# Half-depth products of the first expert layer made full-depth

## The chip, the cores and the metric

The kernel runs on one core of a Trainium2 chip. Its time is the device time of one execution in microseconds (us); runs of the kernel before gave 363.95, 364.14 and 370.61 us, median 364.14. "Faster" and "slower" in this document mean a difference of over 2%.

## The reference: what is computed

Two layers follow each other. First an mLSTM attention over 4 batches, 8 heads, 768 steps and head dimension 40, with a running maximum of the gates, a 40x40 state `C` and a normalizer `n`:

```python
C = f_stab * C + i_stab * einsum('bhd,bhe->bhde', vt, kt)
y[:, :, t] = sigmoid(o_gate) * (C @ qt) / max(|n . qt|, 1)
```

Its result, with heads side by side, is `x` of 4 x 768 rows and 320 columns. Then a gated expert layer:

```python
h = maximum(x @ w_in, 0)            # 320 -> 1024
u, v = h[..., :512], h[..., 512:]
v_n = (v - mean(v)) / sqrt(var(v) + 1e-6)
v_s = einsum('ts,bsd->btd', w_spatial, v_n) + b_spatial[None, :, None]
return (u * v_s) @ w_out            # 512 -> 320
```

The change lies in `x @ w_in`, the first expert layer.

## The kernel before, in words

**High and low parts.** TensorE multiplies a rounded form of float32 here (the type `F32R`). To keep accuracy each operand is split into a high part (a rounded copy) and a low part (what the rounding left): `xH` and `xL` for `x`, `wiH` and `wiL` for `w_in`, and likewise for the spatial weights (`wsH`, `wsL`) and the output weights (`woH`, `woL`). A product of two such operands is the sum of three: high with high, high with low, low with high, all added into one bank of the accumulator memory (PSUM). The product of the two low parts is left out.

**The depth of 320.** The sum over the 320 columns of `x` runs in blocks of 128 rows of the array: two full ones (`j` = 0, 1) and a third of 64 rows. The third is packed: line 655 (`xd`) copies the last 64 columns of `x` beside themselves, so that after the transposes (`px`, line 653) rows 0 to 63 and rows 64 to 127 of the third block of `xH` and `xL` hold the same values. Of the weights, `wiH`'s third block holds for the u half of the layer (columns 0 to 511) high parts in rows 0 to 63 and low parts in rows 64 to 127, and for the v half (columns 512 to 1023) high parts in rows 64 to 127 and low parts in rows 0 to 63. One product of `xH` with all 128 rows so gives two terms at once. The third term, low with high, needs only the 64 rows that hold the high weights. That is the half-depth product, the last of the eight that `a_terms` (line 660) lists.

**Who uses it.** `a_v` (line 675) makes the v half: for each batch and each block of 128 steps one group of eight products of 512 columns into `pm` (line 692), with `x` as the weights that are loaded into the array. `b_u` (line 717) makes the u half: for each batch, each half of the steps and each 128 columns of u one group of eight products of 384 columns into `pu` (line 734), with `w_in` as the loaded weights. That is 24 and 32 groups, so 56 half-depth products in all.

**The rest of TensorE's work.** `s` (line 539) scores, `ex` and `eb` (lines 542, 551) exponents of the gates, `dc` (lines 578, 580) state updates, `pv` (lines 606, 607) the attention's result, `px` transposes, `pb` (lines 744 to 746) the product with the spatial weights, three per block of 128 steps, and `pc` (lines 767 to 769) the output layer. `s`, `dc` and `pv` use narrower tiles of the array: `s` and `dc` 64 x 64, `pv` 128 x 64.

**The order of the work.** The table `ORDER` (lines 49 to 105) lists every task by name, in the order in which it is recorded; each engine runs its own tasks in that order, and semaphores hold back a task whose inputs are not there. `V..` are the `pm` groups, `pu...` the `pu` groups. Attention of later batches runs between the expert layers of earlier ones. DVE (VectorE) and ACT (ScalarE) empty PSUM and make the low parts; POOL (GpSimd) helps with both; SP and ACT issue the transfers. There are eight PSUM banks for all groups.

Of the kernel before, what the change touches and what calls it, by code (L numbers as in the profile page):

```python
# [24 lines left out]
DH = DFF // 2  # L25
# [16 lines left out]
    wiH=([128, 3, DFF], F32R), wiL=([128, 2, DFF], F32R), wsH=([128, 2, NB, 384], F32R), wsL=([128, 2, NB, 384], F32R),  # L42
# [164 lines left out]
class Kernel:  # L207
# [452 lines left out]
    def a_terms(self, b, hf, cx, cw):  # L660
        xH, xL = self.xT[b, hf]
        xH, xL = xH.t, xL.t
        wiH, wiL = self.F("wiH").t, self.F("wiL").t
        for j in range(2):
            yield xH[:, j, cx], wiH[:, j, cw]
            yield xH[:, j, cx], wiL[:, j, cw]
            yield xL[:, j, cx], wiH[:, j, cw]
        yield xH[:, 2, cx], wiH[:, 2, cw]
        r = slice(64, 128) if cw.start >= DH else slice(0, 64)
        yield xL[r, 2, cx], wiH[r, 2, cw]  # L670

    def wi_parts(self, hf):
        return [(self.F("wiH"), (hf, j)) for j in range(3)] + [(self.F("wiL"), (hf, j)) for j in range(2)]
# [164 lines left out]
```

## Time and profile before

| | |
|---|---|
| median of 3 runs | 364.14 us |
| the profiled execution | 364.62 us |
| its span, first to last instruction | 362.8 us |
| TensorE (PE) busy | 345.7 us, 3654 matmuls |
| weight loads (PEld) busy | 300.0 us |
| DVE, ACT, POOL busy | 256.5, 130.7, 108.2 us |

An instruction that the program calls a matmul is two in the trace: a load of the weights into the array (LDWEIGHTS, the PEld rows) and the streaming of the other operand (MATMUL, the PE rows). A load can run beside the matmul ahead of it. The profile models the ends of matmuls, so that neighbouring ones overlap in it, and a PE that reads as always busy may still have air in it. What a matmul costs in a dense stretch is read from the starts: from its own start to the next one's.

### The profile page before, as it was taken

How to read it: one execution, taken by the hardware profiler on the slowest of the kernel's cores; microseconds unless marked ns; L12 is line 12 of the kernel's file. 1: busy time of each engine (PE TensorE's matmuls, PEld its weight loads, DVE VectorE, ACT ScalarE, POOL GpSimd, SP SyncE). 2: the span in 40 equal slices, each digit the busy share in tenths (PEclk: the TensorE clock that was granted, in tenths of full speed). 3: DMA queues.
4: the chain of work that ended last, by engine and by line, in shares of the span. 5: the costliest groups of instructions: out<-in, count | busy, mean ns of one | idle time of the engine just before them, and what ended most of it. 6: DMA issues, size and time to landing. Idle time of an engine off the chain costs nothing.

```text
span 362.8 us, 9069 instructions
## 1 busy us (share of the span) xinstructions
PE 345.7 (95%) x3654; PEld 300.0 (83%) x3654; DVE 256.5 (71%) x545; ACT 130.7 (36%) x312; POOL 108.2 (30%) x154
## 2 busy tenths in 40 slices
PE   0599999999999999999999999999999999999996
PEld 0486877799998978799899878899999788898995
DVE  6899998789978877855487937677847666426362
ACT  2364675851530455622122145630112336302011
POOL 6132635654931042334321006420404412100000
PEclk9999999999999999999999999999999999999999
DMA  7779476966463752513405553160160000100012
GB/s 203 217 216 259 146 199 175 240 150 200 154 178 111 174 117 78 164 33 89 134 18 157 164 98 107 64 176 16 33 152 13 3 0 20 55 2 0 0 38 72
DMA packets 17866, 40.12 MB, mean 111 GB/s; under 512 B 4212, under 2 KB 7860, under 8 KB 17824
## 3 DMA queue, kind: packets, MB, share of 16 engines
q1 hardware_dynamic: 12048, 26.49, 26.9%
q10 hardware_dynamic: 5616, 12.94, 12.9%
q8 instruction: 29, 0.48, 0.6%
q0 software_dynamic: 160, 0.11, 0.2%
q14 instruction: 13, 0.11, 0.1%
HBM read 35.09 MB, written 4.42 MB: 109 GB/s over the span
## 4 chain that ended last, share of the span: by engine, by line
PE 92%; DMA 4%; DVE 2%; POOL 1%; issue 0%; ACT 0%; POOLq 0%; ACTq 0%
PE pm L692 15%; PE pu L734 14%; PE pb L744 11%; PE pb L746 9%; PE pb L745 9%; PE s L539 6%; PE pv L606 6%; PE pc L767 4%; PE dc L578 4%; PE pc L769 4%; PE pc L768 4%; PE px L653 3%; PE ex L542 2%; PE pv L607 1%; DMA GM<-in_gm 1%; DMA GM<-gp 1%
## 5 line engine op out<-in xcount | busy, mean ns | idle before, releaser
L744 PE MATMUL pb<-wsH,v 128*128 128x384 f32 x192 | 68.3, 356 | 0.2 <-DVE KS L255 0.2
L746 PE MATMUL pb<-wsH,v 128*128 128x384 f32 x192 | 64.7, 337 | 0.0
L745 PE MATMUL pb<-wsL,v 128*128 128x384 f32 x192 | 64.7, 337 | 0.0
L744 PEld LDWEIGHTS pb<-wsH,v 128*128 128x128 f32 x192 | 36.1, 188 | 5.6 <-issue 5.4
L539 PE MATMUL s<-QK 40*64 40x64 f32 x768 | 29.6, 233 | 9.7 <-DMA QK<-in_qk 9.7
L255 DVE TENSOR_TENSOR pb<-pb,bsp 128x384 f32<-128x384 f32 x32 | 17.7, 562 | 28.8 <-PE pb L746 28.7
L255 DVE TENSOR_TENSOR KS<-s,W 64x512 f32<-64x512 f32 x48 | 33.0, 687 | 5.6 <-PE s L539 3.3
L745 PEld LDWEIGHTS pb<-wsL,v 128*128 128x128 f32 x192 | 36.2, 189 | 0.3
L746 PEld LDWEIGHTS pb<-wsH,v 128*128 128x128 f32 x192 | 36.1, 188 | 0.0
L734 PE MATMUL pu<-xL,wiH 128*128 128x384 f32 (+1 forms) x96 | 35.5, 370 | 0.0
L539 PEld LDWEIGHTS s<-QK 40*64 40x64 f32 x768 | 26.4, 145 | 10.1 <-DMA QK<-in_qk 9.7
L734 PE MATMUL pu<-xH,wiH 128*128 128x384 f32 x96 | 33.1, 345 | 0.0
L692 PE MATMUL pm<-wiH,xL 128*128 128x512 f32 (+1 forms) x72 | 31.5, 438 | 0.0
L767 PE MATMUL pc<-woH,gt 128*128 128x320 f32 x96 | 31.2, 325 | 0.0
L259 ACT CAST gt<-pb 128x384 fp32r<-128x384 f32 x21 | 10.0, 480 | 58.8 <-DVE pb L255 51.0
L692 PE MATMUL pm<-wiH,xH 128*128 128x512 f32 x72 | 30.4, 422 | 0.0
L255 POOL TENSOR_TENSOR KS<-QK,Eb 64x512 f32<-64x512 f32 (+1 forms) x21 | 27.6, 1316 | 8.6 <-PE pc L769 7.0
L769 PE MATMUL pc<-woH,gt 128*128 128x320 f32 x96 | 29.7, 309 | 0.0
L768 PE MATMUL pc<-woL,gt 128*128 128x320 f32 x96 | 29.7, 309 | 0.0
L606 PE MATMUL pv<-RH,KS 104*64 104x41 f32 x384 | 27.3, 238 | 0.0
L607 PE MATMUL pv<-RH,KS 128*64 128x41 f32 x384 | 27.1, 238 | 0.1
L606 PEld LDWEIGHTS pv<-RH,KS 104*64 104x64 f32 x384 | 25.2, 145 | 2.1 <-issue 1.2
(124 smaller groups left out, 760.2 us busy)
## 6 DMA issues: line engine op xcount, KB each, us to landing
RH<-in_vk SPq DMA_DIRECT2D x35, 256.0 KB
QK<-in_qk SPq DMA_DIRECT2D x15, 448.0 KB
QK<-in_qk ACTq DMA_DIRECT2D x9, 448.0 KB
RH<-in_vk ACTq DMA_DIRECT2D x13, 256.0 KB
out<-o SPq DMA_DIRECT2D x14, 160.0 KB
wsr<-in_w_sp SPq DMA_DIRECT2D x5, 384.0 KB
out<-o ACTq DMA_DIRECT2D x10, 160.0 KB
wir<-in_w_in SPq DMA_DIRECT2D x3, 512.0 KB
```

Source lines behind the costliest of these rows:

```text
L255: return lambda e: e.tensor_tensor(out=out(), in0=in0(), in1=in1(), op=op)
L539: self.nc.tensor.matmul(o[64 - p0:128 - p0, h], q[p0:p0 + D, 0, h], q[p0:p0 + D, 1, h], start=True, stop=True)
L606: self.nc.tensor.matmul(o[0:64, h], ks[0:ke, 0, h], v0[0:ke, h], start=True, stop=True)
L607: self.nc.tensor.matmul(o[64:128, h], ks[:, 1, h], v1[:, h], start=True, stop=True)
L692: self.nc.tensor.matmul(pmt(), l, r, start=i == 0, stop=i == len(terms) - 1)
L734: self.nc.tensor.matmul(put(), w, x, start=i == 0, stop=i == len(terms) - 1)
L744: self.nc.tensor.matmul(pbt(), vH[:, cd], wh[:, s], start=s == 0, stop=False)
L745: self.nc.tensor.matmul(pbt(), vH[:, cd], wl[:, s], start=False, stop=False)
L746: self.nc.tensor.matmul(pbt(), vL[:, cd], wh[:, s], start=False, stop=s == NB - 1)
L767: self.nc.tensor.matmul(pct(), gH[:, c], wh[:, d], start=d == 0, stop=False)
L768: self.nc.tensor.matmul(pct(), gH[:, c], wl[:, d], start=False, stop=False)
L769: self.nc.tensor.matmul(pct(), gL[:, c], wh[:, d], start=False, stop=d == 3)
```

## The change

The half-depth product runs over all 128 rows of the third block. The rows that it now takes in hold the same low parts of `x` and the low parts of the weights, so that low times low is added for these 64 columns of `x`. It holds for both users of `a_terms`.

```diff
@@ a_terms
             yield xH[:, j, cx], wiL[:, j, cw]
             yield xL[:, j, cx], wiH[:, j, cw]
         yield xH[:, 2, cx], wiH[:, 2, cw]
-        r = slice(64, 128) if cw.start >= DH else slice(0, 64)
-        yield xL[r, 2, cx], wiH[r, 2, cw]
+        yield xL[:, 2, cx], wiH[:, 2, cw]
```

The number of instructions stays, and on each engine they stand in the same order. TensorE's instructions wait for the same semaphores at the same places. On the transfer queues a few transfers report to another of the eight completion semaphores than before, and one transfer on ACT's queue and one shift on DVE no longer carry a wait of their own.

## Rows read from the trace of the kernel before

**Rows 1.** The profile's page, totals and the chain that ended last.
```profile
PE 345.7 (95%) x3654; PEld 300.0 (83%) x3654; DVE 256.5 (71%) x545; ACT 130.7 (36%) x312; POOL 108.2 (30%) x154
...
PE 92%; DMA 4%; DVE 2%; POOL 1%; issue 0%; ACT 0%; POOLq 0%; ACTq 0%
```

**Rows 2.** Busy time by stretch: stretch, us, PE, PEld, DVE, ACT, POOL, clock, DMA.
```profile
20.00:50.00 30.00, 29.91 (x456) 22.77 (x456) 28.57 (x60) 17.92 (x44) 13.52 (x15) 1.00 0.80 212
50.00:75.00 25.00, 25.00 (x265) 19.61 (x264) 19.22 (x45) 18.28 (x45) 13.89 (x20) 1.00 0.77 192
75.00:100.00 25.00, 25.00 (x335) 23.54 (x334) 23.87 (x48) 9.64 (x21) 14.94 (x14) 1.00 0.57 169
100.00:125.00 25.00, 25.00 (x314) 22.86 (x312) 20.77 (x51) 6.29 (x15) 4.35 (x6) 1.00 0.54 147
125.00:150.00 25.00, 25.00 (x289) 20.23 (x288) 20.42 (x43) 13.44 (x35) 8.17 (x16) 1.00 0.43 106
```

**Rows 3.** All waits of PE from 50 us to the end: total, times, longest.
```profile
PE pb L744 <- DVE KS L255: 0.2, 1, 0.2
```

**Rows 4.** PE's groups by shape: rows*columns of the tile, moving operand, count, busy, mean ns.
```profile
L734 PE MATMUL pu<-xL,wiH 128*128 128x384 f32 x64 | 21.5, 337 | 0.0
...
L734 PE MATMUL pu<-xL,wiH 64*128 64x384 f32 x32 | 14.0, 436 | 0.0
...
L692 PE MATMUL pm<-wiH,xL 128*128 128x512 f32 x48 | 19.4, 403 | 0.0
...
L692 PE MATMUL pm<-wiH,xL 64*128 64x512 f32 x24 | 12.2, 507 | 0.0
```

**Rows 5.** The same for weight loads; last, idle time before them and what ended it.
```profile
L734 PEld LDWEIGHTS pu<-xL,wiH 128*128 128x128 f32 x64 | 12.0, 188 | 0.0
...
L734 PEld LDWEIGHTS pu<-xL,wiH 64*128 64x128 f32 x32 | 5.9, 183 | 7.9 <-issue 7.9
...
L692 PEld LDWEIGHTS pm<-wiH,xL 64*128 64x128 f32 x24 | 4.5, 187 | 9.0 <-issue 9.0
```

**Rows 6.** Timeline of PE around one `pu` group's end: start us, length us, instruction.
```profile
122.28 0.34 PE L734 MATMUL pu<-xH,wiL 128*128 128x384 f32 x1
122.46 0.33 PE L734 MATMUL pu<-xL,wiH 128*128 128x384 f32 x1
122.63 0.34 PE L734 MATMUL pu<-xH,wiH 128*128 128x384 f32 x1
122.89 0.44 PE L734 MATMUL pu<-xL,wiH 64*128 64x384 f32 x1
123.26 0.44 PE L744 MATMUL pb<-wsH,v 128*128 128x384 f32 x1
123.54 0.34 PE L745 MATMUL pb<-wsL,v 128*128 128x384 f32 x1
123.71 0.34 PE L746 MATMUL pb<-wsH,v 128*128 128x384 f32 x1
```

**Rows 7.** Timeline of the weight loads at the same place.
```profile
122.28 0.19 PEld L734 LDWEIGHTS pu<-xL,wiH 128*128 128x128 f32 x1
122.46 0.19 PEld L734 LDWEIGHTS pu<-xH,wiH 128*128 128x128 f32 x1
122.89 0.18 PEld L734 LDWEIGHTS pu<-xL,wiH 64*128 64x128 f32 x1 [0.25 <-issue]
```

**Rows 8.** Timeline of PE around one `pm` group's end.
```profile
127.42 0.39 PE L692 MATMUL pm<-wiH,xL 128*128 128x512 f32 x1
127.65 0.40 PE L692 MATMUL pm<-wiH,xH 128*128 128x512 f32 x1
127.97 0.50 PE L692 MATMUL pm<-wiH,xL 64*128 64x512 f32 x1
128.40 0.50 PE L692 MATMUL pm<-wiH,xH 128*128 128x512 f32 x1
128.74 0.40 PE L692 MATMUL pm<-wiL,xH 128*128 128x512 f32 x1
```

**Rows 9.** Timeline of PE where a full tile is followed by `dc`.
```profile
77.51 0.34 PE L746 MATMUL pb<-wsH,v 128*128 128x384 f32 x1
77.78 0.23 PE L578 MATMUL dc<-RH 64*40 64x41 f32 x1
```

**Rows 10.** Timeline of PE in the first `pm` group.
```profile
33.41 0.63 PE L692 MATMUL pm<-wiH,xL 128*128 128x512 f32 x1
33.84 0.63 PE L692 MATMUL pm<-wiH,xH 128*128 128x512 f32 x1
34.40 0.79 PE L692 MATMUL pm<-wiH,xL 64*128 64x512 f32 x1
```

## The prediction, as it was made

> **What bounds the kernel now.** I read the page's totals and its chain of waits first: TensorE is busy 95% of the span, and 92% of the chain that ended last runs over it, with 4% on transfers and 2% on DVE [rows 1]. A busy TensorE need not be a bounding one, since the ends of its matmuls are modelled, so I read its waits next: from 50 us to the end it waits once for another engine, for 0.2 us [rows 3]. So for 310 us every matmul starts as soon as the one ahead of it lets it, and what is saved on TensorE there is saved in the end, until another engine comes too late. Which that could be stands in the table by stretch: DVE, with 28.57 of 30 us in the opening and 23.87 of 25 us from 75 to 100 us, and 19 to 21 of 25 us in the stretches beside that [rows 2]. ACT reaches 18.28 of 25 us, POOL less. In the opening, to 50 us, I take DVE to set the pace, and count a saving on TensorE there as nothing.
>
> **What the half-depth products cost now.** By depth they ought to be no dearer than others. By the groups they are: a product of 384 columns that uses 64 rows shows 436 ns against 337 ns for the same product over 128 rows, one of 512 columns 507 against 403 ns [rows 4]. The loads tell more. A full-depth load starts together with the matmul ahead of it and runs beside it: 122.28 and 122.46 us are starts of a load and of the matmul before the one that it feeds [rows 6, 7]. The half-depth load does not: the loading path stands idle for 7.9 us in all ahead of 32 of them and for 9.0 us ahead of 24, ended by nothing that the profile shows ("issue"), and the load starts together with its own matmul [rows 5, 7].
>
> The price in time comes from the starts. In a `pu` group one product follows the other by 0.17 to 0.18 us (122.28, 122.46, 122.63). Then 0.26 us pass to the half-depth product, 0.37 to the next product, which is full-depth again, and 0.28 to the one behind that, after which the step is 0.17 again [rows 6]. The three steps make 0.91 us where three regular ones make 0.52: **0.39 us too many**. In a `pm` group the regular step is 0.23 us (127.42 to 127.65), and the three are 0.32, 0.43 and 0.34, in all 1.09 against 0.70: again 0.39 us [rows 8]. The excess is the same for 384 and for 512 columns, so it is a fixed price of going to a 64-row tile and back, and no cost per column.
>
> **The change, part by part.** It takes out the 64-row tile at 56 places (32 and 24 by the counts [rows 4]) and puts a 128-row one there, with as many columns and as many loaded columns. Added matmuls, loads, instructions on other engines, bytes: none. The new product's price is not shown as such, but the same operands' product over the full blocks is its twin, 64 and 48 times, at the regular step [rows 4]. So the sum is one of removed excess:
> - 51 of the 56 are followed by work in full tiles, and are not among the first two: 51 x 0.39 = 19.9 us. The next groups on TensorE are mostly `pb`, `pc`, `ex`, `px` or another group of the first layer.
> - Three more, beyond the opening, are followed by narrower tiles (`dc` twice, `pv` once). There a change of tile stays: from a full tile to `dc` 0.27 us pass where 0.17 is regular [rows 9], so 0.10 of front cost remains, and I leave the third step of 0.28 against 0.17 in as well. 3 x (0.39 - 0.10 - 0.10), about 0.19 each, is 0.6 us.
> - The first two (`V00`, at 34.40 us, and `V01`) lie in the opening. The step in the first is 0.43 us, twice the later one for the same 512 columns, so TensorE ran at the lower of its two clock levels there [rows 10], whatever the 1.00 in the stretch's row says [rows 2]; what it wins there DVE has to follow with 1.43 us to spare in 30 us. I count nothing; the upper bound is 2 x 0.4 = 0.8 us.
> - The wider reads wait for nothing new: the product ahead in the same group already reads all 128 rows of the third block of `wiH`, and one task writes all rows of `xL`. The few renumbered completion semaphores concern a few loads and take one wait away on DVE and one on ACT's queue; neither engine is named in a wait of TensorE beyond 50 us but for those 0.2 us [rows 3]. Nothing.
>
> Sum: 20.5 us off TensorE. **What comes late next** is DVE. TensorE will reach 75 us some 3 us earlier, and in the 25 us that follow DVE has 1.13 us of air now [rows 2]. Ahead of it lie 5.78 us of air, behind it 4.23 and 4.58, so DVE can work ahead where its inputs allow. The cost lies between nothing and a loss of all that is saved from 50 to 150 us, at an even spread 20.5 x 100 / 313 = 6.5 us. I take 1.5 us, nearer to the low end, since TensorE waits so little today at a DVE share of 95%.
>
> The profiled execution took 364.62 us: 364.62 - 20.5 + 1.5 = 345.6 us. It stood 0.5 us above the median of the runs, 364.14, so the forecast for a median is **345.1 us**, 5.2% less.
>
> **Rivals.**
> 1. DVE becomes the bound. If from 50 to 150 us the work goes by DVE's pace, the 6.5 us of that stretch are lost, not 1.5: 364.1 - 20.5 + 6.5 = 350.1 us. For it speaks the 23.87 of 25 us; against it that DVE shows 84.3 of 100 us over the whole of it [rows 2].
> 2. No change, 364.1 us: the excess belongs to the third block or to a group's end, not to the number of rows, and stays. Against it stands the product right ahead of the half-depth one, which reads the same block over 128 rows at a regular step from its predecessor, and the load that stands idle only where the tile has 64 rows [rows 5 to 7]. The Trainium skill has a rule that would give this outcome: "TensorE: Matmul & The Clock Gate", section "Why this matters for your kernels", says that a lone matmul of depth 32 takes as long as one of depth 128. By that rule alone depth buys nothing in either direction and the sum is 0; the trace disagrees by 99 and 104 ns in the matmuls' own records [rows 4].
> 3. Slower. A full-depth weight load uses all rows of the array. If it cannot run beside a matmul that uses them too, each of the 56 new loads stands open with its 0.188 us [rows 5], and if the excess stays as in rival 2, that is 56 x 0.188 = 10.5 us: 374.7 us. It decides from the point where less than 0.19 of the 0.39 us is won, that is, under half. Against it: full-depth loads start today with the matmul ahead of the one that they feed [rows 6, 7]. The same page of the Trainium skill, section "The mechanism" under "Packing small matmuls", states that a load overlaps with matmuls in flight only when their row groups differ, which is the rule that speaks against this change; the trace does not bear it out for full-depth loads, as the two starts at 122.46 show.
>
> That the change does not do what it says would need the compiler to split a 128-row product again; the twin products over full blocks are not split [rows 4].
>
> **How the numbers follow.** Forecast 0.82, rival 1 0.12, rival 2 0.03, rival 3 0.03. The least time has every excess gone, the opening's too, and nothing given back: 364.1 - 56 x 0.39 = 342.3 us. Upward the range reaches just past rival 1 and leaves out rivals 2 and 3: 342.3 to 350.8 us. 2%, about what a measurement of this kernel can tell from no change, is 356.9 to 371.4 us; forecast and rival 1 lie below: faster 0.94, same 0.03, slower 0.03.
>
> **What would show it.** In the changed kernel's groups by shape no 64-row `pu` or `pm` product, all `xL` products at 337 and 403 ns; no idle time ahead of their loads, where 16.9 us stand now; steps of 0.17 us through the end of a `pu` group and into `pb`; the first `pb` product's mean down; TensorE's busy time near 325 us. Wrong it would be if the third step kept 0.28 us without a change of tile (then 0.11 x 51 = 5.6 us less is won), or if TensorE's waits for DVE between 50 and 150 us came to over 4 us in all.

## The result, and the profile after

The changed kernel takes 346.65 us (median of 4 runs, 346.24 to 350.07) against 364.33 us of the kernel before: ratio 0.9539, 95% interval 0.9463 to 0.9615. On another chip it took 347.85 against 364.85 us, ratio 0.9537 (0.9521 to 0.9552). The forecast was 345.1 us in a range of 342.3 to 350.8. Single executions of one kernel can take several us longer (370.61 us for the kernel before), and the ratios in this document leave those out.

The profile's page shows TensorE's busy time down by 19.5 us, to 326.2, and nobody else's by more than noise; weight loads rose from 300.0 to 303.7 us [rows 1].

```profile
span 345.2 us, 9069 instructions
...
PE 326.2 (95%) x3654; PEld 303.7 (88%) x3654; DVE 257.6 (75%) x545; ACT 130.7 (38%) x312; POOL 108.7 (32%) x154
```

In the groups by shape (columns as before; lines are one lower, as the change takes one line out) the 64-row products are gone. All 96 and 72 products with `xL` stand in one group each, at the time of the full ones before [rows 4]:

```profile
L733 PE MATMUL pu<-xL,wiH 128*128 128x384 f32 x96 | 32.3, 336 | 0.0
...
L691 PE MATMUL pm<-wiH,xL 128*128 128x512 f32 x72 | 29.0, 403 | 0.0
```

Of their weight loads the idle time ahead, 16.9 us over 56 loads before [rows 5], has gone from the `pu` group; what is left ahead of `pm`, 3.3 us over 72 loads, is no longer put down to "issue":

```profile
L733 PEld LDWEIGHTS pu<-xL,wiH 128*128 128x128 f32 x96 | 18.0, 188 | 0.0
...
L691 PEld LDWEIGHTS pm<-wiH,xL 128*128 128x128 f32 x72 | 13.9, 194 | 3.3
```

The timeline of TensorE at the place of [rows 6], start and length in us, shows one step of 0.17 to 0.18 through the end of the group and into `pb`; the steps of 0.26, 0.37 and 0.28 are gone:

```profile
120.42 0.33 PE L733 MATMUL pu<-xL,wiH 128*128 128x384 f32 x1
120.59 0.34 PE L733 MATMUL pu<-xH,wiH 128*128 128x384 f32 x1
120.76 0.34 PE L733 MATMUL pu<-xL,wiH 128*128 128x384 f32 x1
120.94 0.35 PE L743 MATMUL pb<-wsH,v 128*128 128x384 f32 x1
121.12 0.34 PE L744 MATMUL pb<-wsL,v 128*128 128x384 f32 x1
```

What was given back stands in TensorE's waits. From 50 us to the end there were 0.2 us [rows 3]; now there are 1.7:

```profile
PE pu L733 <- ACT W L554: 0.6, 1, 0.6
PE pv L607 <- DVE gt L255: 0.5, 1, 0.5
PE pv L606 <- DVE gt L255: 0.4, 1, 0.4
PE pb L743 <- DVE KS L255: 0.2, 1, 0.2
```

Ahead of 50 us three waits differ. Before:

```profile
PE s L539 <- DMA QK<-in_qk: 9.7, 1, 9.7
PE dc L578 <- POOL RH L255: 2.3, 1, 2.3
```

After:

```profile
PE s L539 <- DMA QK<-in_qk: 10.2, 1, 10.2
PE dc L578 <- POOL RH L255: 1.6, 1, 1.6
...
PE pv L607 <- DVE RH L255: 0.7, 2, 0.4
```

With 1.3 us at the first `ex` in both, TensorE's waits come to 13.5 us before and 15.5 now, 2.0 more. The span fell by 362.8 - 345.2 = 17.6 us, which is the 19.5 us less of busy time and the 2.0 us more of waits, but for rounding; 20.5 were forecast to leave TensorE.

### The profile page after: what moved, and what is told of

The parts are those of the page before. It is cut to its first block, busy times and chain, and to the rows that moved or that the text cites. A ratio compares the mean times of both kernels' runs of the same rounds, so it can differ in the third digit from the quotient of the medians.

```text
span 345.2 us, 9069 instructions
## 1 busy us (share of the span) xinstructions
PE 326.2 (95%) x3654; PEld 303.7 (88%) x3654; DVE 257.6 (75%) x545; ACT 130.7 (38%) x312; POOL 108.7 (32%) x154
## 4 chain that ended last, share of the span: by engine, by line
PE 71%; DVE 4%; issue 1%; ACT 1%
PE pu L733 11%; PE pm L691 10%; PE pb L743 9%; PE pb L745 8%; PE pb L744 8%; PE pc L766 4%; PE pc L768 4%; PE pc L767 4%; PE pv L606 4%; PE s L539 3%; PE dc L578 2%; PE px L653 2%; DVE pb L255 1%; DVE KS L255 1%; PE pv L607 1%
## 5 line engine op out<-in xcount | busy, mean ns | idle before, releaser
L743 PE MATMUL pb<-wsH,v 128*128 128x384 f32 x192 | 65.6, 342 | 0.2 <-DVE KS L255 0.2
L745 PE MATMUL pb<-wsH,v 128*128 128x384 f32 x192 | 64.7, 337 | 0.0
L733 PE MATMUL pu<-xL,wiH 128*128 128x384 f32 x96 | 32.3, 336 | 0.0
L766 PE MATMUL pc<-woH,gt 128*128 128x320 f32 x96 | 30.5, 318 | 0.0
L768 PE MATMUL pc<-woH,gt 128*128 128x320 f32 x96 | 29.6, 309 | 0.0
L691 PE MATMUL pm<-wiH,xL 128*128 128x512 f32 x72 | 29.0, 403 | 0.0
```

The source lines that it names most:

```text
L691: self.nc.tensor.matmul(pmt(), l, r, start=i == 0, stop=i == len(terms) - 1)
L733: self.nc.tensor.matmul(put(), w, x, start=i == 0, stop=i == len(terms) - 1)
L743: self.nc.tensor.matmul(pbt(), vH[:, cd], wh[:, s], start=s == 0, stop=False)
L745: self.nc.tensor.matmul(pbt(), vL[:, cd], wh[:, s], start=False, stop=s == NB - 1)
L766: self.nc.tensor.matmul(pct(), gH[:, c], wh[:, d], start=d == 0, stop=False)
L768: self.nc.tensor.matmul(pct(), gL[:, c], wh[:, d], start=False, stop=d == 3)
```

## The experiments

Two questions were open. What is the price paid for: the missing rows, the third block, the group's end, or the change of the tile's shape? And what gave 3 of the 20 us back? I count shape changes in the program's order on TensorE: a run is a stretch of matmuls with one tile shape. The kernel before has 174 runs, the changed one 66; full tile, 64 x 128, 64 x 64, 128 x 64 and 32 x 128 are five shapes.

**Two half-depth products, side by side.**

```diff
-        yield xH[:, 2, cx], wiH[:, 2, cw]
         r = slice(64, 128) if cw.start >= DH else slice(0, 64)
+        yield xH[r, 2, cx], wiH[r, 2, cw]
         yield xL[r, 2, cx], wiH[r, 2, cw]
```

> From the kernel before; the xH product of the third block takes 64 rows too and stands right ahead of the half-depth xL product, so each group ends with two half-depth products in a row (the term high times low of the last 64 columns of x is left out). 112 half-depth products, but the tile shape changes as often as before: 174 runs of one shape on TensorE against 66 in the changed kernel. If the price is paid per change of shape (20.7 us for 108 changes, 0.19 us each): 364 us, 362 to 366. If each half-depth product pays by itself (0.39 us): 364 + 56 x 0.39 = 386 us.

Ratio to before 1.017 (1.008 to 1.027), profiled span 367.8 us. By the spans that is 5 us over before, outside the expected 362 to 366, and 17 us under the price per product. The timeline shows why the second one is nearly free:

```profile
126.95 0.33 PE L734 MATMUL pu<-xL,wiH 128*128 128x384 f32 x1
127.21 0.44 PE L734 MATMUL pu<-xH,wiH 64*128 64x384 f32 x1
127.49 0.33 PE L734 MATMUL pu<-xL,wiH 64*128 64x384 f32 x1
127.75 0.44 PE L744 MATMUL pb<-wsH,v 128*128 128x384 f32 x1
128.03 0.34 PE L745 MATMUL pb<-wsL,v 128*128 128x384 f32 x1
128.20 0.34 PE L746 MATMUL pb<-wsH,v 128*128 128x384 f32 x1
```

The steps are 0.26, 0.28, 0.26, 0.28 against a regular 0.17: over it by 0.09, 0.11, 0.09, 0.11, in all 0.40, as for one half-depth product alone (0.39). And the second half-depth product's record has the full ones' length, 0.33 us. So a change of shape costs two things. About 0.09 us pass before the first product of the new shape starts, and 0.11 more before the one behind it. The weight loads at the same place say where the 0.11 go:

```profile
127.20 0.18 PEld L734 LDWEIGHTS pu<-xH,wiH 64*128 64x128 f32 x1 [0.25 <-issue]
127.31 0.19 PEld L734 LDWEIGHTS pu<-xL,wiH 64*128 64x128 f32 x1
```

The first load of the new shape starts with its own product, and the next load 0.11 us later, with a regular 0.18 us to the product that it feeds (127.49). So the 0.11 reads as the first load of a run standing open. The 5 us are not in these steps; they are dealt with below.

**The same two, apart.**

```diff
+        r = slice(64, 128) if cw.start >= DH else slice(0, 64)
+        yield xH[r, 2, cx], wiH[r, 2, cw]
         for j in range(2):
             ...
-        yield xH[:, 2, cx], wiH[:, 2, cw]
-        r = slice(64, 128) if cw.start >= DH else slice(0, 64)
         yield xL[r, 2, cx], wiH[r, 2, cw]
```

> The same 112 half-depth products as with the adjacent pair, the same term left out, but the xH one is the first of its group and the xL one the last. TensorE then has 261 runs of one shape against 174. Price per change of shape: 364 + 87 x 0.19 = 381 us, 378 to 383. Price per half-depth product: 386 us and no difference from the adjacent pair. The difference between the two kernels tells: about 16 us by the first, none by the second.

Ratio 1.069 (1.054 to 1.084), span 390.9 us. Against its twin, with the same products in another order, the span is 23 us longer (19 us by the two ratios), 13 of them behind the first output product (below): the order decides, as the price per change has it. But the size missed, by 10 us against the 381 expected.

**96 rows.**

```diff
-        r = slice(64, 128) if cw.start >= DH else slice(0, 64)
+        r = slice(64, 128) if cw.start >= DH else slice(0, 96)
```

> From the kernel before; in the u half alone the last product of a group takes 96 rows (the low weights of 32 columns come in), the v half stays at 64. The compiler gives the 96-row product the full tile: 111 runs of one shape against 174. Price per change of tile shape: 63 x 0.19 = 12 us less, some 0.5 to 1 given back to waits for DVE: 353 us, 351 to 354, and no idle time ahead of the pu loads. Price by missing rows: half of that, 358 us.

Ratio 0.973 (0.962 to 0.985), span 354.2 us; the four runs took 354.3, 356.0, 360.9 and 364.5 us, the least of them just above the expected 351 to 354. TensorE waits 1.8 us for ACT at `pu` here. With a quarter of the rows unused the `pu` product behaves like a full one, while the `pm` product beside it in the same program keeps its price:

```profile
L692 PE MATMUL pm<-wiH,xL 64*128 64x512 f32 x24 | 12.1, 505 | 0.0
...
L734 PE MATMUL pu<-xL,wiH 96*128 96x384 f32 x32 | 10.9, 341 | 0.0
```

The same for the loads:

```profile
L734 PEld LDWEIGHTS pu<-xL,wiH 96*128 96x128 f32 x32 | 6.0, 188 | 0.0
...
L692 PEld LDWEIGHTS pm<-wiH,xL 64*128 64x128 f32 x24 | 4.5, 187 | 9.0 <-issue 9.0
```

**A half-depth product elsewhere.**

```diff
         for j in range(2):
-            yield xH[:, j, cx], wiH[:, j, cw]
+            r = slice(0, 64) if j == 0 else slice(0, 128)
+            yield xH[r, j, cx], wiH[r, j, cw]
```

> From the changed kernel; the first product of each group (xH, block 0) takes 64 rows of its block, so half of that term is left out. The third block stays at full depth. 171 runs of one shape against 66 in the changed kernel. Price per change of shape wherever it stands: 346.7 + 105 x 0.19 = 366.8, less the 2 us of waits that are hidden again: 365 us, 362 to 368. If the excess belonged to the third block or to a group's end: 347 us, 345 to 349.

365.11 us, ratio to before 1.001 (0.999 to 1.004), as expected: the whole gain is gone again, with the third block at full depth. The steps move to the group's start, 0.27, 0.37, 0.28:

```profile
121.84 0.34 PE L746 MATMUL pb<-wsH,v 128*128 128x384 f32 x1
122.11 0.43 PE L734 MATMUL pu<-xH,wiH 64*128 64x384 f32 x1
122.48 0.45 PE L734 MATMUL pu<-xH,wiL 128*128 128x384 f32 x1
122.76 0.34 PE L734 MATMUL pu<-xL,wiH 128*128 128x384 f32 x1
```

**One half of the layer.**

```diff
-        r = slice(64, 128) if cw.start >= DH else slice(0, 64)
+        r = slice(0, 128) if cw.start >= DH else slice(0, 64)
```

> From the kernel before; only the v half (24 groups) goes to full depth, the u half keeps its 64-row product. 129 runs of one shape against 174. Price per change of shape: 45 x 0.19 = 8.6 us less, little given back: 356 us, 355 to 357; together with the u half over 96 rows the two parts then add up to the whole change. If one half of the layer carried all of it: 346 or 364 us.

Ratio 0.986 (0.979 to 0.993), span 360.4, median 359.3, least 357.05 us: the sign was right, the size some 2 us short.

**One rule for all of them.** The misses come from the opening, so I take the stretch behind it: from the first to the last output product (`pc`). The view by tile gives both (durations in ns, then the first and the last start in us). Before:

```profile
L767 PE MATMUL pc<-woH,gt x96: 302/310/418, 94.6 to 358.6; 128*128 128x320 f32 x96
```

After:

```profile
L766 PE MATMUL pc<-woH,gt x96: 302/309/418, 92.8 to 341.0; 128*128 128x320 f32 x96
```

That is 264.0 against 248.2 us, with 116 shape changes against 30 in the program's order from the first `pc` on: 15.8 us for 86 changes, 0.184 us each. The same rows of the other kernels:

| kernel | first to last `pc` | shape changes | 248.2 + 0.184 x (changes - 30) |
|---|---|---|---|
| 96 rows | 95.7 to 350.0: 254.3 | 64 | 254.5 |
| v half alone | 98.0 to 356.2: 258.2 | 82 | 257.8 |
| first product | 94.8 to 359.2: 264.4 | 115 | 263.8 |
| pair adjacent | 99.1 to 363.6: 264.5 | 116 | 264.0 |
| pair apart | 109.0 to 386.7: 277.7 | 187 | 277.1 |

None is off by more than 0.6 us; the changed kernel's second trace, 93.0 to 341.9, is 0.7 us off the first by itself. Rows, blocks and places in the group do not enter. Shown, then: the price is that of changing the tile's shape. It is shown for changes to and from the 64 x 128 tile; the 30 that all these kernels share were not varied.

**The opening.** The pair apart reaches its first `pc` 14.4 us later than the kernel before. Its timeline shows TensorE at 1.2 GHz where the kernel before has long had 2.4: a step of 0.43 us for 512 columns in the second `pm` group, at 46 to 48 us:

```profile
46.48 0.63 PE L692 MATMUL pm<-wiL,xH 128*128 128x512 f32 x1
46.91 0.63 PE L692 MATMUL pm<-wiH,xL 128*128 128x512 f32 x1
47.33 0.63 PE L692 MATMUL pm<-wiH,xH 128*128 128x512 f32 x1
```

The kernel before has that step only in its first `pm` group [rows 10], and 0.23 us in the second. Could the clock be raised early? Two kernels tried it.

```diff
+        def heat():
+            i = F("ident").t
+            for _ in range(28):
+                self.nc.tensor.matmul(self.T(hot)[:, 0:128], i, i, start=True, stop=True)
```

The 28 products are 56 records in the trace.

> From the changed kernel; 28 products of the 128 x 128 identity with itself run on TensorE in its idle time ahead of the first scores (1.3 to 10 us), into a PSUM bank that nobody reads. TensorE works at 1.2 GHz until about 35 us in the changed kernel (512 columns every 0.43 us) and at 2.4 GHz from there on. If dense full-tile work brings the higher level and the narrow tiles after it hold it, the first pm group at 31 us has a step of 0.23 us, and the span falls by 1 to 3 us, no more since DVE sets the pace to 50 us: 343 to 346 us. If the level falls again in TensorE's pauses between 12 and 17 us: no change, 346 to 347 us.

> The kernel with two half-depth products apart (span 390.9 us, TensorE at the lower clock until 64 us) with the same 28 products ahead. If its 10 us over the expected 381 come from the late rise of the clock alone, the rise moves ahead of 36 us and the span falls to 378 to 383 us. If they are the price of the half-depth products themselves: 388 to 391 us.

The first took 349.0 us, ratio 0.955 (0.950 to 0.959), no different from the changed kernel; the second, one run, 394.8 us with a span of 393.0. In both the profile records a change of the clock early, and so the lower level behind it. By stretch (us, then PE, PEld, DVE, ACT, POOL, granted clock, DMA) in the changed kernel with the 28 products:

```profile
0.00:7.00 7.00, 5.65 (x26) 5.65 (x27) 3.78 (x12) 1.58 (x2) 5.68 (x16) 1.00 0.59 180
7.00:14.00 7.00, 4.88 (x65) 4.58 (x63) 6.07 (x15) 2.01 (x4) 0.00 (x0) 0.99 0.98 239
14.00:34.00 20.00, 18.42 (x209) 13.91 (x210) 18.70 (x39) 11.94 (x29) 6.15 (x7) 0.50 0.79 224
34.00:50.00 16.00, 15.08 (x315) 12.36 (x314) 15.43 (x31) 9.71 (x24) 8.58 (x11) 0.99 0.76 199
```

The pair apart with them:

```profile
34.00:50.00 16.00, 16.00 (x179) 12.03 (x178) 11.83 (x24) 6.21 (x15) 7.08 (x8) 0.50 0.59 148
50.00:64.00 14.00, 14.00 (x145) 9.94 (x143) 6.42 (x15) 4.34 (x11) 3.09 (x5) 0.50 0.52 134
66.00:80.00 14.00, 14.00 (x130) 9.54 (x132) 9.49 (x26) 7.93 (x19) 5.15 (x7) 1.00 0.42 121
```

To 7 us, 26 records of the dense products take 5.65 us, 0.21 to 0.22 us each; behind 7 us they follow each other by 0.11. So the 1.00 of the first row is no granted level yet; that of the second is. The level was lost again by 14 us, behind a pause of TensorE of 2.06 us:

```profile
13.83 0.74 PE L549 MATMUL ex<-GM,AT 84*128 84x512 f32 x1 [2.06 <-DMA AT<-ap]
```

The next rise came about when it came without the products. My test of the 10 us failed in that the rise did not move; but it shows the level itself at 0.50 until 64 us, while behind the first `pc` this kernel takes what the pair apart took (110.8 to 388.8 us: 278.0 against 277.7). So the 10 us lie in the opening. Of the 14.4 us there, the 16 shape changes that the pair apart has more ahead of its first `pc` are 2.9 us, an estimate by the rule; the other 11 or so fall into the stretch that it runs at the lower clock. That the clock costs all of them is what is left, and not shown: no run here raised it early and kept it. The 5 us of the adjacent pair lie in the opening too: its first `pc` starts 4.5 us later than before, and the rest takes the same. So does the miss of the v half, whose first `pc` starts at 98.0 us, 3.4 us later than before.

**What gave the gain back.** The new wait at `pu` names an exponent on ACT (`W`), which frees the PSUM bank; ahead of it on ACT's queue stands a square. At `pv` the profile names DVE.

```diff
-... po00 sq01 W6 rh6_0 ...
+... po00 W6 sq01 rh6_0 ...
-... gh000 xl6 dc8 dc9 q8_1 s9 th8 c1_8 ws10_ld ...
+... gh000 dc8 dc9 c1_8 xl6 q8_1 s9 th8 ws10_ld ...
```

> From the changed kernel; two moves in the order table: the exponent W6 ahead of the square sq01 on ACT, and the state sum c1_8 ahead of the low part xl6 on DVE. If the new waits at pu000 (0.9 us) and at pv7 and pv8 (1.0 us) come from these two places, both shrink to under 0.3 us and the span falls by 1 to 1.8 us against the changed kernel: 345 us. If DVE as a whole is the limit there, the waits move to the next product and the time stays at 346.5 us.

348.73 us, ratio 0.958 (0.954 to 0.963): not told from the changed kernel (347.85 us on the same chip); its span is 345.0 against 345.2 us. Its waits of TensorE from 50 us on:

```profile
PE pv L606 <- DVE gt L255: 0.4, 1, 0.4
PE pv L606 <- DVE xL L255: 0.3, 1, 0.3
PE pb L743 <- DVE KS L255: 0.2, 1, 0.2
```

The wait for ACT is gone, so its place is shown. The two waits for DVE, one ahead of each `pv` task, are still there: 0.4 us ahead of the first as before, 0.3 instead of 0.5 ahead of the second, where the profile now names the low part `xL`. So the place of the state sum accounts for 0.2 us at most. It fits DVE being late as a whole between 85 and 93 us, where its instructions follow each other without a pause; but no run here took work off DVE, so this is not shown. No version here beats the changed kernel by more than can be measured.

## Why the prediction was right

- **The bound** was read rightly: TensorE's saving came out as time, 17.6 of 20.5 us.
- **The price of 0.39 us per product**, from three steps in the timeline, held: the steps are gone in the profile after, and they come back wherever a 64-row tile is put. That it is fixed and not per column or row is what the rule above shows on five kernels, with 0.184 us for a change, 0.37 for going and coming back. The 0.39 was read at two places and is a little high. Over the 54 products that it was summed for that is about 1 us, an estimate from the 0.37; TensorE's busy time fell by 19.5 us where 20.5 were forecast.
- **The three with narrower neighbours** were rightly priced lower: each takes out one change of shape and not two. So does `V01` in the opening, which is followed by `eb` (32 x 128): 108 changes go in all, and not 112.
- **The opening** was counted as nothing, and little came of it: 0.7 us of new waits for DVE at `pv` stand against the saving of its two products, and the first `pu` product starts at 50.2 us against 50.7. The clock at its lower level, read from a step of 0.43 us against a row that says 1.00, is borne out by the recorded 0.50.
- **What is given back** was mis-sized, 1.5 us, put down to DVE from 75 us on. It is the 2.0 us by which TensorE's waits grew: 0.9 us for DVE at `pv` at 90 and 92 us, 0.7 for DVE in the opening, 0.6 for ACT at `pu` (0.9 on the loading path), which I had not seen since ACT looked idle on the mean, less 0.2 in the first waits, where `QK` landed 0.5 us later and `dc` waited 0.7 less. The 1.5 us had been chosen between 0 and 6.5 and not worked out, and less than half of what came is what they stood for; that they come so near is partly luck.
- **The 1.5 us** between 345.1 and 346.65 are these two sizes: about 1.0 from the price, 0.5 from what is given back.
- **Rival 1** did not come: DVE shows 87.7 of 100 us from 50 to 150 us and holds TensorE back for 0.9 us there. **Rival 3** did not either: the full-depth loads run beside the matmul ahead, with 0.0 us of idle time ahead of the 96 of `pu`.
- **Rival 2** I dismissed with a wrong word. I wrote that the trace disagrees with the rule that a lone matmul of depth 32 takes as long as one of depth 128 ("TensorE: Matmul & The Clock Gate" of the Trainium skill, section "Why this matters for your kernels"). It does not: 64 rows behind 64 rows take 0.33 us and 96 rows 341 ns. The 99 and 104 ns [rows 4] belong to the first product after a change of shape. That the excess stays with the third block or the group's end is refuted by the half-depth product put at the group's start: 365.11 us with a full-depth third block.

The rule that fits is in the Trainium skill, "TensorEngine Tiling (Array Packing)", section "Key Properties": changing the tiling mode, not just the tile, drains TensorE. The traces agree in the 0.09 us that pass ahead of the new shape, and show 0.11 us more at the first load of it; a drain as such stands in no row.

## What to carry to other kernels

Count the changes of tile shape on TensorE in program order, and price each at its step in the timeline, here 0.18 to 0.20 us; a product that uses fewer rows saves nothing by itself and costs two changes if it stands alone among full ones. Pad it to the full tile with rows that add a harmless or a useful term, or put products of one shape side by side. Read the price from the starts on both sides of the change, since half of it stands with the next instruction, where a table by line hides it.

## What the runs showed of the hardware beyond that

In every trace kept TensorE starts at 1.2 GHz although the profile shows a clock of 1.00 from the first stretch: it records the clock only from its first change on, and the step of 512 columns, 0.43 or 0.23 us, is the surer witness. In the kernels before and after the clock rose in or right behind the first `pm` group, the first stretch of dense full tiles (at 34 to 36 us); in the adjacent pair in the second (at 46 us); in the pair apart and its warmed twin not before 64 us, in the `pu` group behind the third. Half-depth products are not needed for a late rise: the v half at full depth has none in its `pm` groups, ran the first one wholly at 1.2 GHz, and rose only ahead of the second, among the scores, which have narrow tiles: pairs of them follow each other by 0.11 us until 45.2 us and by 0.06 from there on. The steps of 512 columns on both sides, the last of the first stretch and the first of the next:

```profile
35.59 0.63 PE L692 MATMUL pm<-wiH,xL 128*128 128x512 f32 x1
36.01 0.63 PE L542 MATMUL ex<-GM,AT 84*128 84x512 f32 x1
...
46.00 0.40 PE L692 MATMUL pm<-wiL,xH 128*128 128x512 f32 x1
46.23 0.39 PE L692 MATMUL pm<-wiH,xL 128*128 128x512 f32 x1
46.46 0.39 PE L692 MATMUL pm<-wiH,xH 128*128 128x512 f32 x1
```

What sets the time of the rise stays open. Dense products from 1.3 to 10 us raised the clock within their own stretch, and it fell again by 14 us, after a pause of TensorE.
